# Combined rows kept in bf16 in the input's rows, with a new order of the instructions behind the first combination

## The chip, the cores and the metric

The kernel runs on one core of one Trainium2 chip. The core has five engines that each work through their own queue of instructions in order: TensorE (PE, matmuls, with PEld for its weight loads), VectorE (DVE), ScalarE (ACT), GpSimd (POOL) and SyncE (SP, which here only issues DMAs). 16 DMA engines move the data. The metric is the device time of one launch in microseconds (us), lower is better. Each time is the median of several runs.

## What is computed

The reference, cut to what matters:

```python
def _A_ref(q, k, v, shift_k, ssm_k, ssm_D):
    k_shift = ...                      # causal convolution of k over 4 tokens
    kv = k_shift * v
    kv_f = rfft2(pad(kv));  kf_f = rfft2(pad(ssm_k))
    y = irfft2(kv_f * kf_f)[:, :S]     # a long convolution over 2048 tokens
    y = y + kv * ssm_D
    return q * y

def _B_ref(x, w1, b1, w2, b2):
    h = _layernorm(x, axis=-1)
    u = gelu(einsum("bsd,sf->bdf", h, w1) + b1)
    y = einsum("bdf,fs->bds", u, w2) + b2
    return y.transpose(0, 2, 1)

x = A_q                                                  # (1, 2048, 448), bf16
h = x + _A_ref(_layernorm(x), A_k, A_v, A_shift_k, A_ssm_k, A_ssm_D)
h2 = h + _B_ref(_layernorm(h), B_w1, B_b1, B_w2, B_b2)   # w1: 2048x1792, w2: 1792x2048
```

B's layernorm is applied to a row that has been normalized already (`_layernorm(h)`, then again inside `_B_ref`); the kernel folds the two into one normalization with a corrected variance.

## The kernel before

The 2048 tokens are laid out as 128 partitions x 16 rows, token = 16 q + r; a "row" r below is the 128 x 448 tile of the tokens with that r. All data live in one SBUF allocation, the arena, at offsets chosen by hand, so most operands are called `arena`; PSUM has 8 banks, `ps`.

Up to about 75 us the kernel loads k, v and q, makes kv, and does both forward transforms (stages k1, k2, u1, u2) and the first step of the inverse one (i1). i1's results go from SBUF to SBUF by DMA into TZ (line 1201, and 1190 for the last of them), in the order in which the second step wants them: for each of the 16 columns j one transfer for rows 0 to 13 (mostly issued by POOL) and a small one of 28 KB, here called a *tail*, for rows 14 and 15 (mostly issued by SP). A matmul of row 14 or 15 waits for all tails.

The part that the change touches comes then.

- `emit_i2` (line 1281 on): for each row r the second inverse step, two matmuls (line 1300; rows 0 and 1 have four more, line 1308); a gate on ACT or DVE (lines 1315 to 1321, rows 4 to 15), which writes the f32 tile A in TZ's place; the combination (line 1327 for rows 4 to 15, line 1337 for rows 0 to 3), which makes the row of h from A, or from PSUM, and x, and writes A in f32; its statistics (bn_stats for rows 0 and 1, line 1343; a sum in the combination and a square on ACT, line 1355, for the others, then small steps on POOL, lines 1365 to 1379); and the normalization on DVE (line 1386), which writes Q in bf16. From row 8 on a row's matmuls wait for the gate of the row before.
- `emit_mlp`: 7 PSUM banks accumulate the first half of w1's product over all 16 rows (line 1433; `mlp.r` is row r's 7 matmuls, each needs Q of that row), then the second half (line 1443, 112 matmuls), with a gelu behind each group of 16; then w2's product, 14 matmuls a row (line 1455), and the last sum with A and the bias (line 1458), which writes the output row into X, and a store.
- The weights: w1a (line 1406, four loads of 896 KB, the first early), w1b (line 1410, four loads of 896 KB), w2 (line 1417, four loads of 1.5 and 2 MB). All are issued by SP, as are most tails. A load starts when its place in the arena is free.

The order is written out by hand, as the table `ORDER` at the top: a string of tokens for each engine. A token is *step:items*; a step is a stage's name with a running number, the items are the operations in it. `_Sched` checks dependences from byte ranges in the arena, gives each operation a place in its engine's queue by these strings, picks PSUM banks with a model of durations, and puts in the semaphore waits. The tokens that are used below:

| token | what it is |
|---|---|
| i2.1, i2.2 / i2.9, i2.10 | matmuls of rows 0 / 1 |
| i2.17, i2.20, i2.28, i2.32, i2.41, i2.45 | matmuls of rows 2, 3, 4, 5, 6, 7 |
| i2.54, i2.58, i2.67, i2.71, i2.80, i2.84, i2.93, i2.97 | matmuls of rows 8 to 15 |
| i2.3, i2.11, i2.18, i2.21 | combinations of rows 0 to 3 (DVE) |
| i2.29, i2.33, i2.42, i2.46, i2.55, i2.59, i2.68, i2.72, i2.81, i2.85, i2.94, i2.98 | gates of rows 4 to 15 (ACT or DVE) |
| i2.30, i2.34, i2.43, i2.47, ... | combinations of rows 4, 5, 6, 7, ... (DVE) |
| i2.19, i2.22, i2.31, i2.35, ... | squares of rows 2, 3, 4, 5, ... (ACT) |
| i2.8, i2.16, i2.26, i2.27, ... | normalizations of rows 0, 1, 2, 3, ... (DVE) |
| ct.1:7, ct.1:8 | the last transpose (PE) and the copy (ACT) of the table for rows 8 to 11 |
| xn.4, xn.5 | norms of x's rows 2 and 3 (ACT) |
| i1.1, i1.4, ..., i1.16 on SP | TZ's transfers; among them the tails i1.4:19, i1.4:21, i1.8:20, i1.8:22, i1.10:20, i1.10:22, i1.12:20, i1.12:22, i1.14:22 |
| w1a.0 to w1a.3, w1b.0:0-3, w2.0:0-3 | the weight loads (SP) |

Of the kernel before, what the change touches and what calls it, by code (L numbers as in the profile page):

```python
# [6 lines left out]
ACT = mybir.ActivationFunctionType  # L7
# [31 lines left out]
        "mlp.30:0-13 mlp.31:0-13 mlp.32:0-13 mlp.33:0-13 mlp.34:0-13 mlp.35:0-13 mlp.36:0-13 mlp.37:0-13 "
        "mlp.38:0-13 mlp.39:0-10 mlp.39:16-17 mlp.39:11 mlp.39:18-20 mlp.39:12 mlp.39:21-22 mlp.39:13 mlp.39:23-29 "  # L40
# [7 lines left out]
        "xn.2:0 i1.16:18 i1.16:9 ct.2:8 ct.0:8 xn.4:0 ct.1:8 xn.5:0 i2.29:0 i2.46:0 i2.19:0 i2.33:0 i2.22:0 i2.42:0 "  # L48
        "i2.31:0 i2.59:0 i2.35:0 i2.68:0 i2.44:0 i2.48:0 i2.72:0 i2.57:0 i2.81:0 i2.61:0 i2.70:0 i2.74:0 i2.94:0 "
        "i2.83:0 i2.87:0 i2.96:0 i2.100:0 mlp.16:0 mlp.16:4 mlp.16:2 mlp.16:1 mlp.16:5 mlp.16:3 mlp.16:6 mlp.17:16 "  # L50
        "mlp.18:16 mlp.19:16 mlp.20:16 mlp.21:16 mlp.22:16 mlp.23:16 mlp.39:15 "
# [10 lines left out]
        "i2.11:0 i2.5:0 i2.12:0 i2.6:0 i2.18:0 i2.21:0 q.7:3 i2.13:0 i2.8:0 i2.14:0 i2.55:0 i2.30:0 i2.16:0 q.7:1 "  # L62
        "i2.34:0 i2.43:0 i2.26:0 i2.27:0 i2.47:0 q.8:0 q.8:2-3 q.8:1 i2.39:0 i2.56:0 i2.60:0 i2.40:0 i2.69:0 "
        "i2.52:0 i2.53:0 i2.85:0 i2.73:0 i2.65:0 i2.66:0 i2.82:0 i2.86:0 i2.98:0 i2.78:0 i2.99:0 i2.95:0 i2.79:0 "
        "i2.92:0 i2.91:0 i2.104:0 i2.105:0 mlp.24:14 mlp.25:14 mlp.26:14 mlp.27:14 mlp.28:14 mlp.29:14 mlp.30:14 "
        "mlp.31:14 mlp.32:14 mlp.33:14 mlp.34:14 mlp.35:14 mlp.36:14 mlp.37:14 mlp.38:14 mlp.39:14 mlp.39:30 "
# [9 lines left out]
        "q.2:5 xn.3:0 q.4:4-5 q.6:4-5 i2.7:0 i2.23:0-1 i2.15:0 i2.23:2 i2.24:0 i2.25:0 i2.36:0-2 i2.37:0 i2.49:0 "  # L76
        "i2.38:0 i2.49:1-2 q.8:4 i2.50:0 q.8:5 i2.51:0 i2.62:0-2 i2.63:0 i2.64:0 i2.75:0-2 i2.76:0 i2.77:0 "
        "i2.88:0-2 i2.89:0 i2.90:0 i2.101:0-2 i2.102:0 i2.103:0 i2.0:0 "
# [6 lines left out]
        "i1.16:20 i1.16:19 w1a.1:0 i1.12:22 i1.4:21 i1.4:19 w1a.2:0 i1.14:22 i1.10:20 i1.10:22 w1a.3:0 i1.8:22 "  # L85
        "i1.12:20 i1.8:20 w1b.0:0-3 w2.0:0-3 mlp.25:15 mlp.27:15 mlp.29:15 mlp.31:15 mlp.33:15 mlp.35:15 mlp.37:15 "
# [497 lines left out]
def _build(nc, A_q, A_k, A_v, A_shift_k, A_ssm_k, A_ssm_D, B_w1, B_b1, B_w2, B_b2, out):  # L584
# [11 lines left out]
    DB = 2 * D  # L596
# [42 lines left out]
    with ctx:  # L639
# [6 lines left out]
        def view(off, shape, dtype=bf16):  # L646
            size = 4 if dtype in (f32, i32) else 2
            n = 1
            for s_ in shape:
                n *= s_  # L650
            ap = AR[:, off // 2: off // 2 + n * size // 2]
            if dtype is not bf16:
                ap = ap.bitcast(dtype)
            if len(shape) == 2:
                ap = ap.rearrange("p (a b) -> p a b", b=shape[1])
            elif len(shape) == 3:
                ap = ap.rearrange("p (a b c) -> p a b c", b=shape[1], c=shape[2])
            return ap
# [54 lines left out]
        def Pb(b, i=0):  # L713
            return PS[:, b.slots[i], 0:D]
# [569 lines left out]
        def emit_i2():  # L1284
# [5 lines left out]
            for g, (r0, ng) in enumerate(GR):  # L1290
                oh = o_hst + 64 * g
                hs = view(oh, [16], f32)
                for i in range(ng):
# [31 lines left out]

                    def comb(e, W, r=r, A=A, acc=None):
                        return e.scalar_tensor_tensor(out=A, in0=X[:, r, :], scalar=qs[:, r, 0:1], in1=A,  # L1327
                                                      op0=ALU.subtract, op1=ALU.mult,
                                                      **({} if acc is None else {"accum_out": acc}))
                    rx = tz + [(o_X + r * DB, DB), (o_qst + 16 * r, 16)]  # L1330
                    bx = []
                    if r < NX:
                        rx = [(o_TK + r * 4 * D, 4 * D), (o_qx + 8 * r, 8)]
                        bx = [b]

                        def comb(e, W, r=r, A=A, b=b, acc=None):
                            return e.scalar_tensor_tensor(out=A, in0=Pb(b), scalar=qx[:, r, 0:1], in1=XN[:, r, :],
                                                          op0=ALU.add, op1=ALU.mult,
                                                          **({} if acc is None else {"accum_out": acc}))
                    if ng == 1:  # L1340
                        kc = op("dve", comb, r=rx, w=tz, br=bx, n=D, est=640.0 if bx else 595.0)
                        sch.t0 += 0.01
                        op("dve", lambda e, W, hs=hs, A=A: e.bn_stats(out=hs[:, 8:14], in_=A),
                           r=tz, w=[(oh + 32, 24)], n=D, kind="1x")
                        sch.t0 += 0.01
                        agg = op("dve", lambda e, W, hs=hs: e.bn_aggr(out=hs[:, 0:2], in_=hs[:, 8:14]), r=[(oh + 32, 24)],
                                 w=[(oh, 8)], n=6)
                        mv = [(oh, 4), (oh + 4, 4)]
                        mean, var, rst = hs[:, 0:1], hs[:, 1:2], hs[:, 2:3]
                        o_r = oh + 8  # L1350
                    else:
                        kc = op("dve", lambda e, W, hs=hs, i=i, comb=comb: comb(e, W, acc=hs[:, i:i + 1]), r=rx,
                                w=tz + [(oh + 4 * i, 4)], br=bx, n=D, est=650.0 if bx else 605.0)
                        sch.t0 += 0.01
                        op("act", lambda e, W, hs=hs, A=A, i=i: e.activation(out=JK, in_=A, func=ACT.Square,  # L1355
                                                                             scale=1.0 / math.sqrt(D),
                                                                             accum_out=hs[:, 2 + i:3 + i]),
                           r=tz, w=[(oh + 8 + 4 * i, 4), (o_JK, DB)], n=D, est=580.0)
# [23 lines left out]
                for i in range(ng):  # L1382
                    r = r0 + i
                    A = view(o_TZ + r * 2 * DB, [D], f32)
                    sch.t0 += 0.01
                    k = op("dve", lambda e, W, mean=mean, rst=rst, i=i, r=r, A=A: e.tensor_scalar(
                        out=Q[:, r, :], in0=A, scalar1=mean[:, i:i + 1], scalar2=rst[:, i:i + 1],
                        op0=ALU.subtract, op1=ALU.mult),
                       r=[(o_TZ + r * 2 * DB, 2 * DB), mv[0], (o_r, 4 * ng)], w=[(o_Q + r * DB, DB)], n=D, est=428.0)
# [37 lines left out]
        def emit_mlp():  # L1427
# [21 lines left out]
            for r in range(R):  # L1449
                sch.t0 = T_M1 + 90.0 + 3 * r  # L1450
                A = view(o_TZ + r * 2 * DB, [D], f32)
                for d0, d1 in ((0, D),) if r < R - 1 else ((0, 320), (320, D)):
                    b = _Buf(psum)
                    for fc in range(NFC):
# [3 lines left out]
                    op("dve", lambda e, W, r=r, b=b, A=A, d0=d0, d1=d1: e.scalar_tensor_tensor(  # L1458
                        out=X[:, r, d0:d1], in0=Pb(b)[:, d0:d1], scalar=bm[:, r:r + 1], in1=A[:, d0:d1], op0=ALU.add, op1=ALU.add),
                       r=[(o_bm, 64), (o_TZ + r * 2 * DB, 2 * DB)], w=[(o_X + r * DB + 2 * d0, 2 * (d1 - d0))], br=[b],  # L1460
# [57 lines left out]
```

## Time and profile before

| | |
|---|---|
| runs before | 172.63, 172.17, 172.58 us; median 172.58 |
| the profiled execution | 172.93 us |
| its span, from the first to the last instruction | 171.0 us |
| granted TensorE clock, mean | 0.999 |
| PE, DVE, ACT, POOL busy | 95%, 59%, 54%, 36% of the span |
| first matmul of i2 | 74.90 us |
| first matmul of mlp.0 | 80.71 us |
| first matmul of line 1443 | 104.61 us |
| first matmul of line 1455 | 125.8 us |
| last weight load (w2) lands | about 115.4 us |

Busy time is an average over stages with different limits; what sets the time of a stage is seen in the waits of that stage. Waits are put down to the event that came last before an instruction began. Times in a view count from the start of the span. In a table of stretches each row has a stretch of time, its length, the busy time and instruction count of PE, PEld, DVE, ACT and POOL, the granted clock, the mean busy share of the DMA engines and their GB/s. In a timeline each row has a start, a length, the engine, the line, the operation, output and input, and how many were merged; an SP entry is the issue of a DMA, not its transfer.

### The profile page before, as it was taken

Reading aid. Unit: us, or ns where it says so; the run is one execution under the profiler, and the core shown is the slowest. Engines: PE = TensorE matmul, PEld = TensorE weight load, DVE = VectorE, ACT = ScalarE, POOL = GpSimd, SP = SyncE. Lnnn points to the kernel's source line nnn. Section 1 sums busy time; section 2 is a strip of 40 time slices with the busy share of each in tenths; the row PEclk is TensorE's granted clock in tenths of the full one; section 3 lists DMA queues with packets and bytes.
Section 4 is the critical chain, followed back from the end, with each engine's and each line's share of the span. In section 5 each row is a group of like instructions: output and inputs, shape, how many; then the busy total and the mean of one; then the engine's idle time right before and its main releaser. Section 6 shows DMA issues by size and latency. Waiting matters only on the chain.

```text
span 171.0 us, 3573 instructions
## 1 busy us (share of the span) xinstructions
PE 162.3 (95%) x1425; PEld 95.4 (56%) x1425; DVE 101.5 (59%) x188; ACT 92.5 (54%) x132; POOL 61.2 (36%) x154
## 2 busy tenths in 40 slices
PE   6989999989889999988999999999999999999994
PEld 2775845442334434453455555555567777777783
DVE  7988988869899999999989830000003223132231
ACT  3599788988999999989866527321210000000000
POOL 8344827590820576566888830000000000000000
PEclk9999999999999999999999999999999999999999
DMA  5999587675849857657999999960000111101111
GB/s 160 412 293 386 179 275 279 234 295 202 265 126 362 298 174 199 190 164 220 356 370 399 418 421 419 416 273 0 0 0 4 54 54 54 54 0 58 54 54 54
DMA packets 15612, 35.15 MB, mean 206 GB/s; under 512 B 3756, under 2 KB 9724, under 8 KB 15596
## 3 DMA queue, kind: packets, MB, share of 16 engines
q1 hardware_dynamic: 12540, 28.39, 45.8%
q0 software_dynamic: 2912, 6.45, 11.9%
q8 instruction: 11, 0.18, 0.4%
q10 hardware_dynamic: 144, 0.08, 0.2%
q14 instruction: 5, 0.04, 0.1%
HBM read 22.05 MB, written 1.84 MB: 140 GB/s over the span
## 4 chain that ended last, share of the span: by engine, by line
PE 61%; ACT 19%; DVE 12%; DMA 5%; issue 1%; SPq 0%; POOL 0%; DVEq 0%
PE ps L1455 25%; PE ps L1433 13%; PE ps L1443 12%; ACT arena L739 9%; DMA arena<-arena 5%; ACT arena L1070 5%; DVE arena L1161 5%; DVE arena L1237 4%; PE ps L1095 3%; ACT arena L848 2%; PE ps L1060 2%; PE ps L1026 2%; PE ps L967 2%; ACT arena L740 2%; PE ps L1300 2%; PE ps L993 1%
## 5 line engine op out<-in xcount | busy, mean ns | idle before, releaser
L1458 DVE SCALAR_TENSOR_TENSOR arena<-ps,arena 128x448 bf16<-128x448 f32 (+2 forms) x17 | 11.1, 656 | 56.9 <-PE ps L1455 56.9
L1455 PE MATMUL ps<-arena 128*128 128x448 bf16 (+2 forms) x238 | 42.7, 342 | 0.0
L1455 PEld LDWEIGHTS ps<-arena 128*128 128x128 bf16 x238 | 33.3, 145 | 9.5
L739 ACT CAST arena<-ps 128x896 bf16<-128x896 f32 x30 | 24.6, 1016 | 0.2 <-PE ps L1095 0.2
L1433 PE MATMUL ps<-arena 128*128 128x448 bf16 x112 | 22.5, 353 | 0.5 <-DVE arena L1375 0.5
L1070 ACT CAST arena<-ps 128x896 bf16<-128x896 f32 x24 | 20.5, 915 | 3.2 <-PE ps L1060 3.2
L1076 POOL DMA_DIRECT2D arena<-arena x32 | 17.5, 553 | 11.9 <-ACT arena L1070 9.8
L1443 PE MATMUL ps<-arena 128*128 128x448 bf16 x112 | 21.4, 353 | 0.0
L1423 ACT ACTIVATE arena<-ps,arena 128x448 bf16<-128x448 f32 x14 | 8.3, 634 | 18.8 <-PE ps L1443 14.7
L1095 PE MATMUL ps<-arena 128*64 128x448 bf16 x128 | 15.2, 359 | 2.3 <-ACT arena L739 0.8
L1433 PEld LDWEIGHTS ps<-arena 128*128 128x128 bf16 x112 | 10.7, 98 | 11.2 <-DVE arena L1375 0.9
L1161 DVE TENSOR_TENSOR arena<-arena 128x1792 bf16<-128x1792 bf16 x16 | 16.7, 1087 | 0.3 <-ACT arena L739 0.2
L1443 PEld LDWEIGHTS ps<-arena 128*128 128x128 bf16 x112 | 11.0, 98 | 10.2
L1060 PE MATMUL ps<-arena 128*32 128x448 bf16 x256 | 15.0, 355 | 0.8 <-DVE arena L1008 0.5
L1178 PE MATMUL ps<-arena 64*128 64x448 bf16 x128 | 14.5, 351 | 0.1
L1201 POOL DMA_DIRECT2D arena<-arena x15 | 8.8, 592 | 13.2 <-ACT arena L739 13.2
L1095 PEld LDWEIGHTS ps<-arena 128*64 128x64 f16 x128 | 5.8, 108 | 10.7 <-ACT arena L739 2.9
L1178 PEld LDWEIGHTS ps<-arena 64*128 64x128 f16 x128 | 6.1, 94 | 8.2 <-ACT arena L739 2.5
L1008 DVE TENSOR_TENSOR arena<-ps,arena 128x512 bf16<-128x512 f32 (+1 forms) x16 | 9.1, 618 | 1.8 <-PE ps L993 1.6
L1355 ACT ACTIVATE arena<-arena 128x448 bf16<-128x448 f32 x14 | 8.0, 573 | 3.9 <-DVE arena L1327 3.8
L739 ACT COPY arena<-ps 128x1024 bf16<-128x1024 bf16 (+1 forms) x8 | 8.1, 1058 | 3.6 <-PE ps L967 3.5
L1060 PEld LDWEIGHTS ps<-arena 128*32 128x32 f16 x256 | 5.1, 95 | 7.6 <-DVE arena L1008 2.5
(97 smaller groups left out, 197.2 us busy)
## 6 DMA issues: line engine op xcount, KB each, us to landing
arena<-in_B_w_dram SPq DMA_DIRECT2D x8, 896.0 KB, 6.5
arena<-in_B_w_dram SPq DMA_DIRECT2D x2, 2048.0 KB, 17.1
arena<-arena POOLq DMA_DIRECT2D x32, 112.0 KB, 3.3
arena<-arena SPq DMA_DIRECT2D x16, 224.0 KB, 3.6
arena<-in_B_w_dram SPq DMA_DIRECT2D x2, 1536.0 KB, 19.2
arena<-arena POOLq DMA_DIRECT2D x13, 196.0 KB, 4.4
arena<-in_A_k_dram SPq DMA_DIRECT2D x4, 448.0 KB, 5.8
arena<-in_A_v_dram SPq DMA_DIRECT2D x4, 448.0 KB, 9.6
```

Of the source, the lines that this page charges most:

```text
L739: return e.copy(out=dst(), in_=src())
L1008: return e.tensor_tensor(out=v, in0=u.rearrange("p t (r d) -> p t r d", d=64), in1=v, op=ALU.mult)
L1060: op("pe", lambda e, W, b=b, r=r, q=q, x=x, c0=c0: e.matmul(PS[32 * q:32 * q + 32, b.slots[x], 0:D], E[:, 2 * r + x, c0:c0 + 32], src[:, r ...
L1070: return e.copy(out=dst, in_=Ppair(b)) if W == "act" else e.tensor_copy(out=dst, in_=Ppair(b))
L1076: shuf[tag].append(op(q_, lambda e, W, g=g, i=i, a=a, nu=nu, jh=jh: e.dma_start(T[a + i:a + i + 4 * nu - 3:4].rearrange("p (j k) c d -> p ...
L1095: op("pe", lambda e, W, b=bs[h], h=h, j=j, c=c, par=par: e.matmul(PS[64 * par:64 * par + 64, b.slots[c], 0:D], FW[:, 64 * c:64 * c + 64], ...
L1161: op("dve", lambda e, W, m=m, i=i: e.tensor_tensor(out=MR(m.slots[0]).rearrange("p (x y) d -> p x y d", x=2), in0=TU[:, i].unsqueeze(2).br ...
L1178: k = op("pe", lambda e, W, b=bs[h], m=ms[h], par=par, t=t, tab=tab, xy=xy, P=P: e.matmul(Pb(b, par), tab[P, :], MR(m.slots[0])[P, xy, :], ...
L1433: op("pe", lambda e, W, r=r, fc=fc, b=bs[fc]: e.matmul(Pb(b), W1A[:, r, 128 * fc:128 * fc + 128], Q[:, r, :], start=(r == 0), stop=(r == R ...
L1443: op("pe", lambda e, W, r=r, fc=fc, b=b: e.matmul(Pb(b), W1B[:, r, 128 * (fc - n0):128 * (fc - n0) + 128], Q[:, r, :], start=(r == 0), sto ...
L1455: op("pe", lambda e, W, r=r, fc=fc, b=b, d0=d0, d1=d1: e.matmul(Pb(b)[:, d0:d1], W2[fc // 7][:, fc % 7, r:S:R], G[:, fc, d0:d1], start=(fc ...
L1458: op("dve", lambda e, W, r=r, b=b, A=A, d0=d0, d1=d1: e.scalar_tensor_tensor(out=X[:, r, d0:d1], in0=Pb(b)[:, d0:d1], scalar=bm[:, r:r + 1 ...
```

## The change

The model's durations for some operations, the byte ranges and the tile that these operations use are changed, in `emit_i2` and `emit_mlp`: the combination writes X's row (bf16), in the place of the f32 tile A in TZ; bn_stats, the square, the normalization and the last sum read X's row. The gate still writes A in f32.

```diff
                     def comb(e, W, r=r, A=A, acc=None):
-                        return e.scalar_tensor_tensor(out=A, in0=X[:, r, :], scalar=qs[:, r, 0:1], in1=A,
+                        return e.scalar_tensor_tensor(out=X[:, r, :], in0=X[:, r, :], scalar=qs[:, r, 0:1], in1=A,
                                                       op0=ALU.subtract, op1=ALU.mult,
...
-                        def comb(e, W, r=r, A=A, b=b, acc=None):
-                            return e.scalar_tensor_tensor(out=A, in0=Pb(b), scalar=qx[:, r, 0:1], in1=XN[:, r, :],
+                        def comb(e, W, r=r, b=b, acc=None):
+                            return e.scalar_tensor_tensor(out=X[:, r, :], in0=Pb(b), scalar=qx[:, r, 0:1], in1=XN[:, r, :],
...
-                        op("dve", lambda e, W, hs=hs, A=A: e.bn_stats(out=hs[:, 8:14], in_=A),
+                        op("dve", lambda e, W, hs=hs, r=r: e.bn_stats(out=hs[:, 8:14], in_=X[:, r, :]),
...
-                        op("act", lambda e, W, hs=hs, A=A, i=i: e.activation(out=JK, in_=A, func=ACT.Square,
+                        op("act", lambda e, W, hs=hs, r=r, i=i: e.activation(out=JK, in_=X[:, r, :], func=ACT.Square,
...
-                        out=Q[:, r, :], in0=A, scalar1=mean[:, i:i + 1], scalar2=rst[:, i:i + 1],
+                        out=Q[:, r, :], in0=X[:, r, :], scalar1=mean[:, i:i + 1], scalar2=rst[:, i:i + 1],
...
-                       r=[(o_TZ + r * 2 * DB, 2 * DB), mv[0], (o_r, 4 * ng)], w=[(o_Q + r * DB, DB)], n=D, est=428.0)
+                       r=[(o_X + r * DB, DB), mv[0], (o_r, 4 * ng)], w=[(o_Q + r * DB, DB)], n=D, est=311.0)
...
-                        out=X[:, r, d0:d1], in0=Pb(b)[:, d0:d1], scalar=bm[:, r:r + 1], in1=A[:, d0:d1], op0=ALU.add, op1=ALU.add),
+                        out=X[:, r, d0:d1], in0=Pb(b)[:, d0:d1], scalar=bm[:, r:r + 1], in1=X[:, r, d0:d1], op0=ALU.add, op1=ALU.add),
```

And the strings of `ORDER` are other ones from the first combination (i2.3) on. PE's begins to differ behind row 1, ACT's behind ct.0, DVE's behind i2.6, POOL's behind i2.7, SP's behind i1.16:19. The start of each, and all of SP's:

```diff
 pe
-i2.28:0-1 i2.17:0-1 i2.45:0-1 i2.20:0-1 i2.41:0-1 i2.32:0-1 i2.54:0-1 mlp.0:6 mlp.0:1 mlp.0:5 mlp.0:2-4 mlp.0:0
-i2.58:0-1 mlp.1:6 mlp.1:0 mlp.1:4 mlp.1:3 mlp.1:2 mlp.1:1 mlp.1:5 i2.67:0-1 mlp.2 (7) i2.71:0-1 mlp.3 (7)
-i2.80:0-1 mlp.4 (7) mlp.5 (7) i2.84:0-1 mlp.6 (6) i2.93:0-1 mlp.6:2 mlp.7 (7) i2.97:0-1 mlp.8 (7) ...
+i2.45:0-1 i2.17:0-1 i2.32:0-1 i2.28:0 i2.54:0-1 i2.20:0-1 i2.28:1 i2.41:0-1 i2.58:0-1 mlp.0:3 mlp.0:0 mlp.0:6
+mlp.0:2 mlp.0:5 mlp.0:4 mlp.1:5 mlp.1:4 mlp.0:1 mlp.1:2-3 mlp.1:6 mlp.1:1 mlp.1:0 i2.67:0-1 mlp.2 (7) i2.71:0-1
+mlp.3 (7) i2.80:0-1 mlp.4 (7) i2.84:0-1 mlp.5 (7) i2.93:0-1 mlp.6 (7) mlp.7 (4) i2.97:0-1 mlp.7 (3) mlp.8 (7) ...
 act
-xn.4:0 ct.1:8 xn.5:0 i2.29:0 i2.46:0 i2.19:0 i2.33:0 i2.22:0 i2.42:0 i2.31:0 i2.59:0 i2.35:0 i2.68:0 ...
+ct.1:8 xn.4:0 i2.46:0 xn.5:0 i2.55:0 i2.19:0 i2.29:0 i2.22:0 i2.33:0 i2.59:0 i2.31:0 i2.35:0 i2.68:0 ...
 dve
-i2.18:0 i2.21:0 q.7:3 i2.13:0 i2.8:0 i2.14:0 i2.55:0 i2.30:0 i2.16:0 q.7:1 i2.34:0 i2.43:0 i2.26:0 i2.27:0 ...
+i2.13:0 i2.18:0 i2.14:0 i2.21:0 i2.8:0 i2.42:0 q.7:3 i2.16:0 i2.30:0 i2.34:0 q.8:2 i2.26:0 i2.27:0 ...
 pool
-i2.23:0-1 i2.15:0 i2.23:2 i2.24:0 i2.25:0 ...
+i2.15:0 i2.23:0-2 i2.24:0 i2.25:0 ...
 sp
-w1a.1:0 i1.12:22 i1.4:21 i1.4:19 w1a.2:0 i1.14:22 i1.10:20 i1.10:22 w1a.3:0 i1.8:22 i1.12:20 i1.8:20 w1b.0:0-3 w2.0:0-3
+i1.4:21 i1.4:19 w1a.1:0 i1.12:22 i1.12:20 i1.14:22 w1a.2:0 i1.8:20 i1.10:22 i1.10:20 w1a.3:0 w1b.0:0-3 i1.8:22 w2.0:0-3
```

(A number in brackets stands for all or so many of a row's seven matmuls, whose order among themselves is left out.) No operation is added or taken away.

## The prediction

> **What bounds the kernel now.** I read the engine table of the page first, then the chain that ended last, the stretches behind the first combination, and the queue that SP feeds.
>
> ```profile
> PE 162.3 (95%) x1425; PEld 95.4 (56%) x1425; DVE 101.5 (59%) x188; ACT 92.5 (54%) x132; POOL 61.2 (36%) x154
> ```
> ```profile
> 1.38 3.54 PE ps L1026 x9
> ...
> 80.25 0.40 DVE arena L1386
> 80.65 0.07 DVE arena L1375
> 80.72 1.48 PE ps L1433 x7
> ...
> 94.19 10.59 PE ps L1433 x56
> 104.78 21.19 PE ps L1443 x112
> 125.97 42.08 PE ps L1455 x231
> ```
>
> The chain (start, length, what) is TensorE alone from 80.72 us on: 112 matmuls of L1443 in 21.19 us, 0.189 us each. Nothing but more matmul time or a PE that waits can move the end.
>
> ```profile
> 74.80:80.70 5.90, 5.31 (x27) 2.44 (x27) 5.71 (x20) 5.05 (x9) 3.38 (x5) 1.00 0.56 170
> 80.70:84.20 3.50, 3.49 (x19) 1.57 (x20) 3.50 (x12) 3.19 (x9) 3.05 (x7) 1.00 1.04 358
> 84.20:104.60 20.40, 20.40 (x109) 10.55 (x109) 13.94 (x37) 11.34 (x27) 13.61 (x31) 1.00 1.04 400
> ```
>
> In these stretches (us, then PE, PEld, DVE, ACT, POOL busy, granted clock, DMA share, GB/s) PE is full from 80.70. From the first second-inverse matmul at 74.90 (timeline) to the first of L1443 at 104.61 there are 152 matmuls and one short transpose: 152 x 0.1891 + 0.06 = 28.80 of 29.71 us. So **PE waits 0.9 us in all** behind the first combination (0.18 before row 8, 0.64 for the first normalized row at 80.71, the rest in slivers); that is all a better order can win. The DMA engines, though, are full from 79 to 113 us, with the weights. Who stands where in SP's queue:
>
> ```profile
> 76.94 0.38 SPq L1406 DMA_DIRECT2D arena<-in_B_w_dram  x1
> 77.37 2.11 SPq L1201 DMA_DIRECT2D arena<-arena  x3
> 79.52 0.44 SPq L1406 DMA_DIRECT2D arena<-in_B_w_dram  x1
> 80.00 2.09 SPq L1201 DMA_DIRECT2D arena<-arena  x3
> 82.14 0.44 SPq L1406 DMA_DIRECT2D arena<-in_B_w_dram  x1
> 82.62 2.10 SPq L1201 DMA_DIRECT2D arena<-arena  x3
> 84.76 2.99 SPq L1410 DMA_DIRECT2D arena<-in_B_w_dram  x4
> 87.81 9.85 SPq L1417 DMA_DIRECT2D arena<-in_B_w_dram  x4
> ```
> ```profile
> L1410 SPq DMA_DIRECT2D arena<-in_B_w_dram x4: 374/476/1131, 84.8 to 87.4; - x4
> ...
> DMA to landing us min/median/max: 6.3/8.4/10.3
> ```
>
> The first view shows all nine L1201 tails (28 KB each, rows 14 and 15 of one column of TZ) issued before w1b (L1410). The second: w1b's four loads land 6.3 to 10.3 us after issue, each later than the one before; the last, issued at 87.38, lands at 97.7. **SP's transfers are served in the order of issue.** The tails show it too, in the trace's landing events: those issued at 77.37, 78.10 and 78.81, behind w1a.1, land at 82.00, 82.24 and 82.45, just behind that load's last event at 81.93; one issued at 61.22, with no load ahead, took 2.4 us.
>
> **The change, part by part.**
>
> Types. The combination (L1327 674 ns, L1337 676) keeps its inputs and only writes bf16. L1458 has a bf16 output and takes 684, so nothing; nor does the trace hold a faster two-input row with an f32 operand. bn_stats: 628 (L1343, f32) becomes 609 (L1237, bf16), twice. Q's normalization (L1386, 507 ns, f32 in) gets a bf16 input; the nearest SBUF rows are the casts of 128 elements, 278 ns for 32-bit and 211 for 16-bit, so 211 to 507, and I take 390, about three quarters as the casts have it; 16 x 0.12 = 1.9 us of DVE, of which 6.5 us are idle from 84.20 to 104.60 anyway. The square on ACT (573) and the last sum (L1458) keep their rows: the first has no 16-bit form faster than it (L1270, 16-bit in, 844), the second lies behind PE, idle 56.9 us. On PE's path only the first normalized row counts, some 0.14 us.
>
> Order of ACT, DVE, PE. By the trace's durations ACT's copy ct.1 is put ahead of the norm of row 2; the norm ran at 76.08, the copy waits for a transpose that ends at 76.44, so ACT begins 0.40 us later and the square of row 3 ends at about 81.85 in the place of 81.36. On DVE the first normalized row starts at 80.16 as before (two combinations still stand ahead of it) and ends 0.12 earlier. PE does row 9 before mlp.0 now, but its row 8 waits for the gate of row 7 to 78.80 (0.25 us), and mlp.0's seventh accumulator for the gate of row 5. PE stands at mlp.2 at about 84.1 us; before it was 84.17. Bounds: 0.9 us won (no wait left) and some 0.5 lost (row 3's square, 0.49 late, with no faster normalization). I take 0.
>
> SP's queue. Two tails (i1.4:21, i1.4:19) move ahead of w1a.1, into SP's gap from 74.80 to 76.94: nothing. The others move ahead or stay, w1b starts right behind w1a.3 at 82.6 instead of 84.76, and **i1.8:22 moves behind all four loads of w1b.** That tail is needed by row 14, i2.93, which PE has between mlp.5 and mlp.6; PE runs in order, so mlp.6 and everything after waits with it.
>
> - When row 14 is due: 36 matmuls of rows 0 to 13 and 42 of mlp.0 to mlp.5 from 74.90: 78 x 0.1891 + 0.06 + 0.9 of waits = 90.6 us.
> - When the tail lands: w1b's last load landed at 97.7. Three tails no longer stand between w1a.3 and w1b; in the landing events each costs the queue 0.25 us: 97.0. Bounds: 98.0 (nothing won, plus one tail's 0.25), and 95.4: seven loads of 0.918 MB and their tails, 6.65 MB, at the 405 GB/s of the fullest stretch, from 79.0. I take 97.0, the row itself.
> - The wait: 97.0 - 90.6 = 6.4 us. Behind it come 74 matmuls (rows 14, 15, mlp.6 to mlp.15): 14.0 us; then L1443 to the end of the span as before, 171.0 - 104.61 = 66.4. Sum 177.4, against 171.0: **+6.4**. All that PE gains or loses earlier vanishes in this wait; if the wait weren't there, the 0 of the last paragraph (0.9 won to 0.5 lost) would be the result. Row 15's statistics don't end last: before, it took 6.4 us from its matmuls (93.64) to Q (100.0); it comes 13 matmuls behind row 14, so Q is ready at 97.0 + 2.5 + 6.4 = 105.9, and mlp.14 is due 60 matmuls behind row 14, at 108.3. The second half of w1 lands before L1443; w2's third load waits for the same tail, with 17 us and more in hand before L1455.
>
> Clock. In the trace of before PE never idles over 0.6 us in its middle. At the ends it does:
>
> ```profile
> 4.90:6.70 1.80, 1.80 (x22) 1.43 (x20) 1.80 (x5) 0.72 (x1) 0.00 (x0) 1.00 1.02 410
> 6.70:8.00 1.30, 1.30 (x25) 1.11 (x24) 1.04 (x3) 1.23 (x2) 0.59 (x2) 1.00 1.02 416
> ...
> 168.60:170.50 1.90, 0.00 (x0) 0.00 (x0) 0.28 (x2) 0.00 (x0) 0.00 (x0) 1.00 0.22 60
> 170.70:171.00 0.30, 0.00 (x0) 0.00 (x0) 0.00 (x0) 0.00 (x0) 0.00 (x0) 0.50 0.00 0
> ```
>
> At the end the granted clock (third from the right) is 0.50 two us after the last matmul. At the start PE has run since 1.38; L1026's nine matmuls of the same shape as L1443's came 0.373 us apart (instructions read one by one), twice 0.189, and L967's transposes go from 0.107 to 0.056 us apart at 6.7. (The column says 1.00 there; the spacing tells otherwise.) So a wait of 6.4 us is long enough to halve the clock, and what follows is slow until it is granted again: 5.3 us at the start, which at half rate loses 2.65. Bounds: 0 (clock kept, as over every idle stretch of before, 0.59 at most) and 3.4 (5.3 and half as long again, read from one start alone). I take 2.2, near the start's row and less, as PE may meet the release at any point. **Sum: +6.4 + 2.2 = +8.6**, a span of 179.6. The profiled execution took 172.93 with its span of 171.0, 0.35 over the median of 172.58; from the median, **181.2 us**.
>
> [...]
>
> **The rivals.**
>
> *The tail is not held* (not slower). If 28 KB slip past the loads and land by 90.6 us, the point from which this decides, PE meets no wait and no slow clock, and only the early part counts: 0.9 us won at best, 0.5 lost at worst, 172.6 with my 0. For it: the tail uses fewer increments (8 against 16) than a load. Against it: nine tails of this trace landed behind the load ahead of them.
>
> *The wait comes, the clock stays*: 172.6 + 6.4 = 179.0. For it: half a clock shows only before and after the work. Against it: two us of idleness at the end were enough.
>
> *The wait comes and more behind it*: the tail at 98.0 and 3.4 us lost to the clock, or row 15's gate on a full ACT queue making mlp.14 wait: 172.6 + 7.4 + 3.4 = 183.4. For it: the margin before mlp.14 is 2.4 us. Against it: a pair of rows costs ACT 2.9 us at most (two gates of 0.71, two squares of 0.57 and 0.19), and PE 18 matmuls, 3.4 us.
>
> **How the numbers follow.** Forecast 0.60, clock kept 0.20, more behind it 0.08, tail not held 0.12. The forecast's time is 181.2. The range leaves out the tail not held and reaches down to the clock kept with the tail at 95.4 (172.6 + 4.8 = 177.4, of which I cut 0.3) and up to 183.4. About 0.3%, 0.5 us, is what can be told from no change; the tail not held gives 0.05 faster, 0.06 the same, 0.01 slower; all the rest is slower: 0.89.
>
> **What would show it.** In the profile after: PE idle some 6 us ahead of row 14's matmul (line of i2's first matmul, about 90 to 97 us), released by an SBUF to SBUF DMA; clock 0.50 in a stretch behind it and matmuls 0.373 apart; SP issuing one L1201 behind L1410's four; L1443 starting at 112 to 114 instead of 104.6 and, once the clock is back, as long as before, 21.2 us; the normalization at about 390 ns with bf16 in. Wrong would be: no idle stretch over 1 us on PE behind 81 us, or a tail that lands before the load ahead of it has.

## The result, and the profile after

The changed kernel takes 181.77 us (median of six runs, 181.00 to 183.04); the kernel before, beside it, 172.59 us (six runs, 172.17 to 173.10). The ratio is 1.0515, with a 95% interval of 1.0483 to 1.0547: some 9 us slower. The profiled execution took 182.23 us with a span of 180.3 us, against 172.93 and 171.0 before, so +9.3 us in both. (The ratios below leave out runs with a disturbed clock, six of tail_ahead's twelve and two of the 17 of the kernel before beside them, and so need not be the quotients of the medians; the profiled executions of tail_ahead and tail_mid are such runs, with the clock at half for 3.4 us from 13.05 and 14.15 us on, so their totals are not used.)

First the engine table of the changed kernel's page:

```profile
PE 165.2 (92%) x1425; PEld 95.8 (53%) x1425; DVE 99.0 (55%) x187; ACT 93.0 (52%) x133; POOL 59.5 (33%) x154
```

PE has as many instructions as before and is busy 2.9 us longer: the same matmuls, some of them slower. DVE is 2.5 us less busy. Neither explains 9 us. The chain that ended last does (start, length, what):

```profile
85.26 1.32 PE ps L1433 x7
...
87.39 10.10 DMA arena<-arena
97.49 0.05 issue
97.53 0.93 PE ps L1300 x2
...
102.86 11.16 PE ps L1433 x59
114.02 21.19 PE ps L1443 x112
135.21 42.08 PE ps L1454 x231
```

Before, this chain was PE alone from 80.72 us on. Now a transfer from SBUF to SBUF stands in it for 10.10 us, and behind it row 14's two matmuls (L1300). L1443 begins at 114.02 in the place of 104.78, and from there both chains have the same lengths, 21.19 and 42.08 us: all of the loss lies before that line. PE's timeline gives the wait in brackets:

```profile
88.50 1.49 PE L1433 MATMUL ps<-arena 128*128 128x448 bf16 x7
97.53 0.93 PE L1300 MATMUL ps<-arena 128*128 128x448 bf16 x2 [7.54 <-DMA arena<-arena]
```

PE stands idle for 7.54 us, right where mlp.5 has ended and row 14 is due. Who issues the transfer, in SP's timeline (an entry is the issue):

```profile
81.40 0.43 SPq L1406 DMA_DIRECT2D arena<-in_B_w_dram  x1
81.86 5.07 SPq L1410 DMA_DIRECT2D arena<-in_B_w_dram  x4
87.39 1.77 SPq L1201 DMA_DIRECT2D arena<-arena  x1
89.21 9.22 SPq L1417 DMA_DIRECT2D arena<-in_B_w_dram  x4
```

One L1201, the tail i1.8:22, stands alone behind the four loads of w1b. It is issued at 87.39, 2.4 us before row 14 is due, and yet lands at 97.49. The loads ahead of it, by the view of line 1410:

```profile
L1410 SPq DMA_DIRECT2D arena<-in_B_w_dram x4: 518/686/3051, 81.9 to 83.9; - x4
...
DMA to landing us min/median/max: 8.5/11.0/13.3
```

The fourth load, issued at 83.9, lands 13.3 us later, at 97.2; the tail follows it by 0.27 us. What comes behind the wait is seen in the table of stretches, cut where the clock changes (us, length, busy time of PE, PEld, DVE, ACT, POOL, granted clock, DMA share, GB/s):

```profile
88.61:92.02 3.41, 1.38 (x8) 0.49 (x5) 1.43 (x6) 2.73 (x9) 2.76 (x8) 1.00 1.05 403
92.03:95.43 3.40, 0.00 (x0) 0.00 (x0) 0.00 (x0) 0.00 (x0) 2.01 (x7) 0.50 1.06 411
95.44:98.84 3.40, 1.30 (x4) 0.59 (x5) 0.34 (x1) 0.00 (x0) 0.00 (x0) 0.50 1.04 411
98.85:102.25 3.40, 3.40 (x10) 1.37 (x9) 1.56 (x5) 0.67 (x2) 0.49 (x2) 0.50 1.03 387
102.27:105.60 3.33, 3.33 (x19) 1.73 (x18) 1.92 (x6) 1.89 (x5) 1.18 (x3) 1.00 1.03 389
```

The clock falls to half while PE waits and stays there until 102.26. In the fourth row PE is full and gets through 10 matmuls in 3.40 us; in the fifth, at full clock, 19 in 3.33 us. Between 97.53 and 102.26, 4.73 us, PE works at half rate, which loses 2.4 us. In the middle rows the other engines run dry as well, POOL last.

The account, from the first matmul of i2 to the first of L1443:

| | before | after |
|---|---|---|
| first matmul of i2 | 74.90 | 73.88 |
| small waits of PE up to row 14 | 0.9 | 1.1 |
| wait ahead of row 14, beyond a matmul's spacing | 0 | 7.7 |
| lost to the half clock | 0 | 2.4 |
| first matmul of L1443 | 104.61 | 113.86 |
| from the one to the other | 29.71 | 39.98 |

The sum 0.2 + 7.7 + 2.4 = 10.3 is the stage's 39.98 - 29.71 = 10.27 us. The stage began 1.0 us earlier in this execution, which leaves 9.25 of the span's 9.3. (Over all twelve profiled executions here, old order or new, that start lies anywhere from 73.9 to 77.5 us, and nothing ahead of it was changed, so it is not counted as an effect.)

### The profile page after: what moved, and what is told of

The parts are those of the page before. It is cut to its first block, busy times and chain, and to the rows that moved or that the text cites. A ratio compares the mean times of both kernels' runs of the same rounds, so it can differ in the third digit from the quotient of the medians.

```text
span 180.3 us, 3570 instructions
## 1 busy us (share of the span) xinstructions
PE 165.2 (92%) x1425; PEld 95.8 (53%) x1425; DVE 99.0 (55%) x187; ACT 93.0 (52%) x133; POOL 59.5 (33%) x154
## 4 chain that ended last, share of the span: by engine, by line
PE 65%; ACT 17%; DMA 12%; POOL 2%; DVE 1%; issue 1%; SPq 0%; DVEq 0%
PE ps L1454 23%; PE ps L1443 12%; DMA arena<-arena 12%; PE ps L1433 10%; ACT arena L739 8%; ACT arena L1070 5%; PE ps L1095 5%; PE ps L1178 4%; PE ps L1300 3%; ACT arena L848 2%; PE ps L1060 2%; PE ps L1026 2%; PE ps L967 2%; ACT arena L740 1%; PE ps L993 1%
## 5 line engine op out<-in xcount | busy, mean ns | idle before, releaser
L1454 PEld LDWEIGHTS ps<-arena 128*128 128x128 bf16 x238 | 33.3, 145 | 9.5
L1433 PE MATMUL ps<-arena 128*128 128x448 bf16 x112 | 24.5, 374 | 0.2
L1076 POOL DMA_DIRECT2D arena<-arena x32 | 17.6, 554 | 11.9 <-ACT arena L1070 10.3
L1443 PE MATMUL ps<-arena 128*128 128x448 bf16 x112 | 21.4, 352 | 0.0
L1433 PEld LDWEIGHTS ps<-arena 128*128 128x128 bf16 x112 | 11.3, 103 | 12.6 <-issue 2.2
L1443 PEld LDWEIGHTS ps<-arena 128*128 128x128 bf16 x112 | 11.0, 98 | 10.2
L1300 PE MATMUL ps<-arena 128*128 128x448 bf16 x32 | 8.1, 366 | 8.0 <-DMA arena<-arena 7.8
L1201 POOL DMA_DIRECT2D arena<-arena x15 | 8.8, 592 | 13.2 <-ACT arena L739 13.2
L1356 ACT ACTIVATE arena<-arena 128x448 bf16<-128x448 bf16 x14 | 8.0, 572 | 9.7 <-DVE arena L1327 9.5
```

The costliest lines, as they stand in the source:

```text
L1076: shuf[tag].append(op(q_, lambda e, W, g=g, i=i, a=a, nu=nu, jh=jh: e.dma_start(T[a + i:a + i + 4 * nu - 3:4].rearrange("p (j k) c d -> p ...
L1300: k = op("pe", lambda e, W, b=b, r=r, h=h: e.matmul(Pb(b), ET[:, 2 * r + h, :], TZ[:, r, h, :], start=(h == 0), stop=(h == 1 and r >= NZ)) ...
L1433: op("pe", lambda e, W, r=r, fc=fc, b=bs[fc]: e.matmul(Pb(b), W1A[:, r, 128 * fc:128 * fc + 128], Q[:, r, :], start=(r == 0), stop=(r == R ...
L1443: op("pe", lambda e, W, r=r, fc=fc, b=b: e.matmul(Pb(b), W1B[:, r, 128 * (fc - n0):128 * (fc - n0) + 128], Q[:, r, :], start=(r == 0), sto ...
L1454: op("pe", lambda e, W, r=r, fc=fc, b=b, d0=d0, d1=d1: e.matmul(Pb(b)[:, d0:d1], W2[fc // 7][:, fc % 7, r:S:R], G[:, fc, d0:d1], start=(fc ...
```

## The experiments

Ratios are to the kernel before, with 95% intervals; +1% is 1.7 us.

**One token, both ways.** If the place of one tail is the whole loss, putting it back into the changed kernel must bring the time of before, and moving it alone in the kernel before must bring the time of after.

```diff
 sp, of the changed kernel (tail_ahead)
-w1a.3:0 w1b.0:0-3 i1.8:22 w2.0:0-3
+w1a.3:0 i1.8:22 w1b.0:0-3 w2.0:0-3
 sp, of the kernel before (before_tail_late)
-w1a.3:0 i1.8:22 i1.12:20 i1.8:20 w1b.0:0-3 w2.0:0-3
+w1a.3:0 i1.12:20 i1.8:20 w1b.0:0-3 i1.8:22 w2.0:0-3
```

> The changed kernel with one token moved in SP's order: the tail i1.8:22 ahead of w1b's four loads. Theory (the tail waits in SP's queue, PE's clock halves in the wait): row 14 finds its data, PE has no idle stretch over 1 us behind i2's first matmul, the clock stays at 1.00, and the time is that of before but for the early part: 172.6, between 171.7 and 173.1. Rival (the new order of ACT, DVE and PE, or the bf16 rows, cost the time): it stays above 177. Rival (half and half): 174 to 177.

> The kernel before with one token moved in SP's order: the tail i1.8:22 behind w1b's four loads. Theory: row 14 is due at about 91.6 us and its tail lands at 97.5 to 98, so PE waits some 6.2 us, and the clock loses 1 to 3.4 more: 180.5 to 182, with 181.0 the likeliest. Rival (the new order or the bf16 rows cost the time): 172.6.

Measured: tail_ahead 1.0004 [0.9962, 1.0045], and no idle time over 1 us on PE in the stage: row 14's matmuls start as mlp.5's seven end.

```profile
92.09 1.49 PE L1433 MATMUL ps<-arena 128*128 128x448 bf16 x7
93.41 0.54 PE L1300 MATMUL ps<-arena 128*128 128x448 bf16 x2
```

before_tail_late 1.0513 [1.0458, 1.0568], 182.28 us; its PE timeline has the wait at the same instruction:

```profile
91.41 1.30 PE L1433 MATMUL ps<-arena 128*128 128x448 bf16 x6
99.34 0.93 PE L1300 MATMUL ps<-arena 128*128 128x448 bf16 x2 [6.63 <-DMA arena<-arena]
```

So the kernel before, with its own types and all its other orders, is as slow as the changed one (1.0515) once this tail stands behind w1b; and the changed kernel without it is as fast as before. The whole loss is one token, and everything else in the change sums to nothing that can be measured.

**Is the slow clock a cost of its own?** In pe_kept_busy the tail stays late, and 34 matmuls without use stand in PE's queue ahead of row 14. They read the transform's tables and write a PSUM bank that nobody reads; the computation is whole.

```diff
 pe
-... mlp.5:0-4 i2.93:0-1 mlp.6:0 ...
+... mlp.5:0-4 busy.0:0-33 i2.93:0-1 mlp.6:0 ...
+        def emit_busy(n_):
+            b = _Buf(psum)
...
+                op("pe", lambda e, W, b=b: e.matmul(Pb(b), FW, view(o_DR, [D], f16), start=True, stop=True),
+                   r=r_fw + [(o_DR, DB)], bw=[b], n=D)
```

> The changed kernel with 34 matmuls more on PE, which read tables and write a PSUM bank that nobody reads, ahead of row 14's matmuls: 34 x 0.189 = 6.4 us of work inside the 7.5 us of waiting. Theory: the tail lands when it did, at about 97.5, but the clock never halves, so the 2.3 us that were lost at half rate come back: 179.4, and the spread over the runs shrinks. Rival (what follows the wait is slow for another reason, or not slow at all): 181.8 as it was.

Measured: 1.0398 [1.0343, 1.0452]. The stretches across the wait and behind it:

```profile
90.70:97.00 6.30, 6.30 (x35) 3.13 (x32) 1.26 (x4) 1.40 (x5) 3.69 (x11) 1.00 1.05 410
97.00:102.00 5.00, 4.89 (x26) 2.47 (x26) 2.83 (x8) 1.95 (x5) 0.74 (x4) 1.00 1.03 424
```

PE is full through the wait, the clock stays at 1.00, and 26 matmuls go through the 5 us behind it. The tail is still late: it lands at 96.97 by the trace's landing events, and row 14 starts at 97.28, 6.7 us after it was due (7.7 in the changed kernel). The difference of the two ratios, 1.17% or 2.0 us with some 1.1 to either side, is put down to the clock; the rest, about 7 us, is the wait itself. The two profiles say the same: the stage takes 36.6 us in the place of 40.0, and of these 3.3 us 1.0 is the shorter wait and 2.3 the clock. Useless work in the gap thus makes the kernel faster, though far from as fast as before.

**How far back in the queue?** The wait should grow with each load ahead of the tail.

```diff
 sp, of the changed kernel
-w1a.3:0 w1b.0:0-3 i1.8:22 w2.0:0-3
+w1a.3:0 w1b.0:0-1 i1.8:22 w1b.0:2-3 w2.0:0-3
 ... or (tail_later)
+w1a.3:0 w1b.0:0-3 w2.0:0 i1.8:22 w2.0:1-3
```

> The changed kernel with the tail i1.8:22 behind two of w1b's four loads. Theory (served in the order of issue, 2.25 us for each load): it lands 4.5 us earlier, at about 93.0, with row 14 due at 90.0: a wait of 3.0 us. 175.1 if the clock outlives that wait, up to 177.4 if not. Rival (the DMA engines are simply full, whatever the order): 181.8 as it was. Rival (only a place behind all of w1b matters): 172.6.

> The changed kernel with the tail also behind the first of w2's loads, 2.1 MB at some 405 GB/s. Theory (order of issue): it lands 5.2 us later, at about 102.7, PE waits 12.7 us, and the clock loses as much as in the changed kernel: 187, ratio 1.08. Rival (there is a longest time that a small transfer is held): 181.8, ratio 1.05.

PE's timeline of tail_mid and of tail_later, the line of row 14:

```profile
95.63 0.55 PE L1300 MATMUL ps<-arena 128*128 128x448 bf16 x2 [2.06 <-DMA arena<-arena]
```
```profile
102.58 0.93 PE L1300 MATMUL ps<-arena 128*128 128x448 bf16 x2 [10.85 <-DMA arena<-arena]
```

| loads of w1b and w2 ahead of the tail | wait of PE | ratio |
|---|---|---|
| none (tail_ahead) | none over 1 us | 1.0004 [0.9962, 1.0045] |
| two of 896 KB (tail_mid) | 2.06 us | 1.0129 [1.0079, 1.0180] |
| four (the changed kernel) | 7.54 us | 1.0515 [1.0483, 1.0547] |
| four, and one of 2 MB (tail_later, two runs) | 10.85 us | 1.0776 [1.0699, 1.0853] |

From the second row to the third, two loads more cost 5.5 us of wait. At the 411 GB/s of the stretches above, 2 x 0.918 MB take 4.5 us, and by their landings they took 4.6 (92.59 to 97.22 us in the changed kernel), so the bytes ahead explain most of it. The rest is mostly the loads before them: w1b's second landed 16.4 us behind the issue of w1a.1 in the changed kernel and 15.5 in tail_mid.

The sizes were misses: 3.0 us of wait were expected of tail_mid and 12.7 of tail_later. tail_later's load of 2 MB did take the 5 us foreseen (97.72 to 102.76), but its weight loads began 0.5 us sooner behind i2's first matmul, w1b had landed 0.7 us sooner behind their start, and the tail landed 0.2 us ahead of the load's last event in the place of 0.3 behind it. The rival by which there is a longest time that a small transfer is held gets no support: this one took 12.5 us from issue to landing.

The three runs of tail_mid that are compared have a mean clock of 0.999 to 1.000 and are by their ratio some 2.2 us slower than before: a wait of about 2 us, which was traced in another execution, cost them its own length and no more.

**Same lateness, another queue.** Is the tail late because the DMA engines are full, or because of who stands ahead of it in SP's queue? In tail_by_pool POOL issues it, at about the same time as SP does in the changed kernel.

```diff
-for q_, a, b_, j0 in (("sp" if j == 3 else "pool", 0, 112, 0), ("pool" if jj == 2 else "sp", 112, 128, 14)):
+for q_, a, b_, j0 in (("sp" if j == 3 else "pool", 0, 112, 0), ("pool" if jj == 2 or j == 7 else "sp", 112, 128, 14)):
 pool
-... i2.38:0 q.8:4-5 ...
+... i2.38:0 q.8:4-5 i1.8:22 ...
 sp
-w1a.3:0 w1b.0:0-3 i1.8:22 w2.0:0-3
+w1a.3:0 w1b.0:0-3 w2.0:0-3
```

> The changed kernel with the tail i1.8:22 issued by POOL, some 13 us behind i2's first matmul, where SP issued it in the changed kernel; w1b's four loads still go ahead of it in time, but in another queue. Theory (it waited for its turn in SP's queue): it lands some 4 us behind its issue, as POOL's transfers do, about when row 14 is due: at most 1 us of waiting, a clock at 1.00, a ratio of 1.000 to 1.008 to before. Rival (the DMA engines are full, so whatever is issued at that time lands late): lands at about 97, ratio 1.05 as the changed kernel.

POOL's timeline, its DMA view (size, us to landing) and PE's timeline:

```profile
88.35 0.64 POOL L1201 DMA_DIRECT2D arena<-arena  x1
```
```profile
arena<-arena POOLq DMA_DIRECT2D x1, 28.0 KB, 5.0
```
```profile
93.42 0.55 PE L1300 MATMUL ps<-arena 128*128 128x448 bf16 x2 [2.03 <-DMA arena<-arena]
```

Issued at 88.35, 13.1 us behind i2's first matmul (13.5 by SP in the changed kernel), it lands in 5.0 us in the place of 10.1, ahead of two loads of w1b that SP had issued 3.6 and 4.4 us before it (they end at 95.42 and 97.79). The engines were as full, with 400 GB/s in that stretch. So half of the 10 us is the place in SP's queue and not the load on the engines. (The two transfers differ in one thing more: in the traces of before and of the changed kernel each of POOL's L1201 transfers leaves 16 landing events, and a tail of SP 9, eight of them at its end. What that does was not tested.) How the engines let the tail past two bulk loads in 5.0 us is not shown. The size was a miss: at most 1 us of wait and 1.008 were expected, and it came to 2.03 us and 1.0175 [1.0108, 1.0242], since the tail still took 5.0 us beside the loads, where three tails of SP with no load ahead had taken 2.4, 3.0 and 3.1 in the kernel before.

**The types alone.** types_only is the changed kernel's operations under the order of before.

```diff
-out=Q[:, r, :], in0=A, scalar1=mean[:, i:i + 1], scalar2=rst[:, i:i + 1],
+out=Q[:, r, :], in0=X[:, r, :], scalar1=mean[:, i:i + 1], scalar2=rst[:, i:i + 1],
...
 ORDER: as before
```

> The bf16 rows with the order of before on every engine. Theory (types save 0.12 us on the first normalized row, the rest is hidden): PE's stage from i2's first matmul to L1443's first takes 29.6 us, ratio 0.999, not to be told from 1. Rival (the types alone pay, and the new order gives it back): ratio 0.996 or less. Rival (a 16-bit row costs somewhere): over 1.004.

Measured: 0.9993 [0.9959, 1.0028], and by the view of the normalization's line (min, median, max in ns):

```profile
L1386 DVE TENSOR_SCALAR arena<-arena x16: 364/394/405, 80.3 to 100.3; 128x448 bf16<-128x448 bf16 x16
```

With an f32 input the median was 509. The 16 x 0.115 = 1.8 us come off an engine that waits anyway, and the time doesn't move.

**Row 14 later on PE.** Can the order be mended on PE's side? In row14_later the tail stays late, and rows 14 and 15 go behind mlp.11, with their gates and combinations moved back accordingly on ACT and DVE (their squares and normalizations stood last already).

```diff
 pe
-... mlp.5:0-4 i2.93:0-1 mlp.6 (7) mlp.7 (4) i2.97:0-1 mlp.7 (3) ... mlp.11 (7) mlp.12 (7) ...
+... mlp.5:0-4 mlp.6 (7) mlp.7 (7) ... mlp.11 (7) i2.93:0-1 mlp.12 (4) i2.97:0-1 mlp.12 (3) ...
 act
-i2.98:0 i2.87:0
+i2.87:0 i2.98:0
 dve
-i2.94:0 i2.82:0 i2.65:0 i2.66:0 i2.99:0 i2.95:0 i2.78:0 i2.79:0 i2.92:0 i2.91:0 i2.105:0
+i2.82:0 i2.65:0 i2.66:0 i2.78:0 i2.79:0 i2.92:0 i2.91:0 i2.94:0 i2.95:0 i2.99:0 i2.105:0
```

> The changed kernel with its late tail, but with rows 14 and 15 moved back in PE's order behind mlp.11, and their gates, combinations, squares and normalizations moved back on DVE and ACT. Theory (the late tail costs because mlp.6 to mlp.13 stand behind row 14 in PE's queue): PE fills the 7.5 us with 42 matmuls, the clock stays at 1.00, and what is left is the chain from row 14's landing to mlp.14: a wait of 1.4 to 3 us, a ratio of 1.009 to 1.02. Rival (the late tail costs its lateness whatever PE has to do): 1.04 or more.

PE's timeline:

```profile
100.27 0.54 PE L1300 MATMUL ps<-arena 128*128 128x448 bf16 x2
...
101.98 2.05 PE L1433 MATMUL ps<-arena 128*128 128x448 bf16 x10
106.56 2.82 PE L1433 MATMUL ps<-arena 128*128 128x448 bf16 x14 [2.53 <-DVE arena L1386]
```

The wait ahead of row 14 is gone, and the next thing is late in its place: mlp.14 waits 2.53 us for the normalization, which ends 6.3 us behind row 14's matmuls. The ratio is 1.0222 [1.0154, 1.0290], a little over the 1.009 to 1.02 expected. Here the tail landed at 98.53 by the landing events, so row 14 could have stood 1.7 us earlier; by estimate mlp.14 would still have waited some 0.8 us. With the tail this late there is no place on PE that hides both the transfer and the row's own 6.3 us.

**Is there a gain in the early order?** The new order's first stretch has a wait of its own, 0.37 us ahead of row 7's first matmul, and mlp.2 starts 9.51 us behind i2's first matmul where before it started 9.27 behind it. Two attempts: copy_second (tail_ahead, with ACT's copy and norm in the order of before) and early_norms (types_only, with the statistics of rows 0 and 1 ahead of other work).

```diff
 act (copy_second)
-ct.0:8 ct.1:8 xn.4:0 i2.46:0
+ct.0:8 xn.4:0 ct.1:8 i2.46:0
 dve (early_norms, from the order of before)
-i2.6:0 i2.18:0 i2.21:0 q.7:3 i2.13:0 i2.8:0 i2.14:0 i2.55:0 i2.30:0 i2.16:0
+i2.6:0 i2.13:0 i2.18:0 i2.14:0 i2.8:0 i2.21:0 i2.16:0 q.7:3 i2.55:0 i2.30:0
 pool (early_norms)
-i2.23:0-1 i2.15:0 i2.23:2
+i2.15:0 i2.23:0-2
```

> The changed kernel with the tail ahead of w1b and, on ACT, the norm of x's row 2 ahead of the copy ct.1 again. Theory (the 0.37 us that PE waits ahead of row 7, as the changed kernel has it, end with that copy): the copy ends some 0.7 us later and the wait grows to about 1.0 us. Rival (that wait ends with the last of TZ's transfers): it stays within 0.1 us of 0.37, or moves with the landing.

> The bf16 rows with the order of before, but on DVE rows 0 and 1 are normalized as soon as POOL has their roots: the first behind the combination of row 2, the second behind that of row 3, and POOL makes row 1's root ahead of rows 2 and 3's means. Theory: mlp.0 starts 0.5 to 0.6 us earlier behind i2's first matmul than with the order of before, mlp.2 some 0.3, and PE's stage takes 29.2 to 29.5 us in the place of 29.7: a ratio of 0.997 to 0.999, too little to be told from 1 by the time. Rival (row 3's square, and with it mlp.2, is as late as before whatever the first rows do): 29.7.

copy_second (a single execution): the 0.37 us are gone, which neither theory had expected; mlp.2 starts 9.16 us behind i2's first matmul, and the time is 173.07 beside 172.93 of before. early_norms: 1.0025 [1.0001, 1.0050], a shade slower. In its PE timeline mlp.0 begins 5.17 us behind i2's first matmul (5.68 in types_only), and then:

```profile
79.83 1.30 PE L1433 MATMUL ps<-arena 128*128 128x448 bf16 x6
81.39 0.36 PE L1433 MATMUL ps<-arena 128*128 128x448 bf16 x1 [0.26 <-DVE arena L1319]
81.93 0.55 PE L1300 MATMUL ps<-arena 128*128 128x448 bf16 x2 [0.18 <-ACT arena L1317]
```

The 0.5 us won at mlp.0 are given back at its last accumulator, which waits for a PSUM bank that a gate (L1319) still holds, and at the next row, for a gate on ACT; mlp.2 starts at 9.63, and the stage takes 30.1 us in the place of the 29.2 to 29.5 expected. None of these versions beats the kernel before by more than can be told from no change.

## Why the prediction was right

Its likeliest case came true, mechanism and sum: 181.77 us against 181.2 forecast. By its steps:

- **PE bounds.** Confirmed: from L1443 on nothing changed, and the loss is PE's wait and PE's clock.
- **Types, nothing.** Confirmed by types_only at 0.9993. The normalization was taken at 390 ns and has a median of 392; the combination, with medians of 677 and 672 ns (675 and 677 before), gained nothing from its bf16 output, and bn_stats, foreseen at 609 ns, stayed at 627.
- **Order of ACT, DVE and PE, nothing.** Confirmed in sum by tail_ahead at 1.0004; wrong in a detail. The 0.25 us foreseen ahead of row 8 were 0.04; 0.37 us came ahead of row 7, which no step had. copy_second shows that they hang on ACT's copy being ahead of the norm, but not by which dependence: the trace names no event there, and that stays open.
- **The tail behind w1b.** Confirmed by the pair of experiments with one token. The term was mis-sized: 6.4 us of wait foreseen, 7.7 measured beyond a matmul's spacing. Counted from i2's first matmul, the tail was to land 22.1 us later and landed 23.6 later (97.49 - 73.88); row 14 was due 15.7 us later by the sum and 15.95 in the profile; 1.5 - 0.25 is the 1.3 us. Of the 1.5 us, 0.7 are what three tails fewer were to save and did not: the fourth load of w1b lands 20.7 us behind the issue of w1a.1 before (97.68 - 76.94) and 21.0 after (97.22 - 76.22). In the ten experiments it is 20 to 21, so a saving by the tails can't be told from the spread of the loads themselves. The rest is these loads' 0.3 us more, the stream's start, 2.34 us behind i2's first matmul in the place of 2.04, and the tail's own 0.27.
- **The clock.** 2.2 us foreseen from the start's row; 2.4 in the profile and 2.0 (0.9 to 3.1) by the comparison with pe_kept_busy. The rival by which the clock stays falls with that. The upper bound of 3.4 us, which also stands in the range's upper end, is not what the start gives (5.3 us and half as long again is 7.95, and half of that 4.0), and no run shows it: in the four profiles with the half clock behind row 14's wait PE worked at half rate for 3.38 us (tail_mid), 4.5 (tail_later), 4.73 (the changed kernel) and 5.5 (before_tail_late), which loses 1.7 to 2.7.
- **The tail behind the load ahead of it.** Confirmed to within 0.3 us: the tail landed 0.27 us behind the last event of the load, as in before_tail_late. In pe_kept_busy, row14_later and tail_later it landed ahead of that event, but by 0.21, 0.08 and 0.23 us only. In these five profiles the wait on SP's queue went by the place in it, to within some 0.3 us, and on another queue (tail_by_pool, 5.0 us past two loads) it did not. One reading of the prediction is wrong here: not all nine tails of before landed behind the load ahead of them. The three behind w1a.3 landed at 87.98, 88.16 and 88.34, ahead of its last event at 88.82. So the order of issue is what these traces show for SP's transfers, with landings up to 0.84 us out of it, and not a rule.
- **Row 15 and mlp.14 not late.** Confirmed: behind row 14 there is no wait on PE. With rows 14 and 15 moved back (row14_later) that margin is gone, and mlp.14 waits 2.53 us for 6.3 us of statistics; the prediction had 6.4.

That the median is only 0.6 us above the forecast is in part luck: in the profiled execution the wait came out 1.3 us longer, and the stage began 1.0 us earlier.

## What to carry to other kernels

Here a transfer's size said little about when it landed: 28 KB issued 2.4 us ahead of its use came 7.5 us late, because four bulk loads stood ahead of it in the same queue. So for each small transfer that a matmul waits for, add up the bytes ahead of it in its queue, and issue it ahead of bulk loads or through another queue, if that is fast enough (here, beside the loads, 5.0 us in the place of 10.1). Where an engine runs in order and another sets its pace, an order found for it has to be judged with the backlog of the DMA queues in mind: the rest of this change, types and order, made no difference that could be measured, and one token cost 9 us.

## What the hardware showed unexpectedly

**The half clock came in multiples of 3.41 us, and fell with PE only partly idle.** It lasts 10.24 us in the changed kernel's profile, three times 3.41, and 6.83, twice that, in before_tail_late. In the changed kernel the clock fell at 92.02, only 2.0 us after PE's last matmul; the 3.41 us that ended there (88.61 to 92.02, in the first table of stretches) still had 1.38 us of work. Cut into stretches of the same length, counted from the changes of the clock, before_tail_late, tail_later and tail_mid (its 3.4 us at half are one such stretch):

```profile
91.19:94.60 3.41, 1.52 (x9) 0.53 (x6) 2.80 (x8) 1.57 (x6) 2.77 (x8) 1.00 1.04 399
94.61:98.00 3.39, 0.00 (x0) 0.00 (x0) 1.09 (x4) 0.00 (x0) 1.98 (x4) 1.00 1.06 411
98.02:101.42 3.40, 2.08 (x6) 0.89 (x7) 0.00 (x0) 1.11 (x3) 0.00 (x0) 0.50 1.03 423
101.43:104.83 3.40, 3.40 (x10) 1.37 (x9) 0.79 (x2) 0.82 (x4) 1.11 (x3) 0.50 1.03 424
```
```profile
90.03:93.44 3.41, 1.70 (x9) 0.69 (x7) 1.75 (x6) 3.05 (x9) 2.76 (x8) 1.00 1.05 404
93.45:96.84 3.39, 0.00 (x0) 0.00 (x0) 0.00 (x0) 0.00 (x0) 2.35 (x7) 1.00 1.06 414
```
```profile
92.66:96.06 3.40, 1.34 (x8) 0.54 (x7) 1.30 (x4) 2.26 (x7) 2.78 (x7) 1.00 1.05 404
96.08:99.46 3.38, 3.38 (x11) 1.39 (x10) 1.90 (x5) 0.67 (x2) 2.40 (x8) 0.50 1.06 414
```

Stretches with 1.34 and 1.38 us of PE's work were followed by the half clock, and stretches with 1.52 and 1.70 us were not: there it fell one stretch later. In these profiles it went back up only behind a stretch full of work (3.38 and 3.40 us); one with 2.08 us did not do it. PE's busy time alone does not decide it, though. Early in the span, where most of PE's instructions are smaller, tail_mid's clock fell behind a stretch with 2.50 us of work, and tail_later's did not behind one with 2.46:

```profile
10.74:14.15 3.41, 2.50 (x34) 2.16 (x33) 2.27 (x8) 3.41 (x4) 0.00 (x0) 1.00 1.02 336
14.15:17.56 3.41, 3.41 (x34) 1.54 (x33) 2.10 (x4) 1.70 (x3) 1.80 (x4) 0.50 1.06 378
```
```profile
8.10:11.52 3.42, 2.46 (x27) 1.77 (x27) 3.42 (x6) 3.42 (x4) 2.53 (x3) 1.00 1.04 291
```

So no threshold can be read from these traces, and what sets the 3.41 us is not shown. Nor is the time at half the same in each run of the changed kernel: the mean clock is 0.972 in two of the six, among them the profiled one with its 10.24 us, and 0.980 or 0.981 in the other four, by estimate from the mean some 6.8 us at half. In tail_mid's profile the clock halved between 96.06 and 96.08 behind a wait of 2.06 us that lay whole in one such stretch (92.66 to 96.06). In tail_by_pool's profile a wait as long, 2.03 us, lay across two (counted back from its last change of clock in steps of 3.413 us, a third of the 10.24; that the steps run on so is the author's assumption), with 2.06 and 2.73 us of work, and the clock stayed:

```profile
89.33:92.74 3.41, 2.06 (x11) 0.88 (x9) 1.97 (x7) 3.12 (x9) 2.74 (x9) 1.00 1.05 403
92.74:96.15 3.41, 2.73 (x15) 1.46 (x16) 2.05 (x7) 0.73 (x3) 2.91 (x8) 1.00 1.05 400
```

**Issuing took long too.** In the changed kernel SP spent 3.05 us on the issue of one load of w1b (1.13 at most before) and 1.77 us on the tail, where three tails together took it 2.09. Why is not shown: before, the issues of w2's loads took up to 3.76 us, and in row14_later the tail's took 0.69 us behind the same four loads.
